# Where the constants lie in SBUF: the fp32 identity moved behind all other constants, and the transposed k's tiles rounded up to 128 bytes

## The chip, the core and the metric

The kernel runs on one core of a Trainium2 chip. Five engines run side by side, each with its own instruction stream: TensorE (PE, with its weight loads shown as PEld), VectorE (DVE), ScalarE (ACT), GpSimd (POOL) and SyncE (SP). They share the on-chip memory SBUF (128 partitions) and, but for GpSimd and the DMAs, the accumulators in PSUM. Data moves between HBM and SBUF by 16 DMA engines, which work on transfers that POOL, SP and ACT issue. The metric is the time of one execution in microseconds (us), measured on the device; the median of several runs counts.

## The reference

Sparse attention with 8 heads, of which four see the last 32 positions ("local") and four see every 32nd position ("strided"), and then a feed-forward layer with ELU.

```
q, k, v: (8 batches, 8 heads, 576 positions, 64), fp32
scores = q k^T / 8
local  heads 0-3: 0 <= i - j < 32
strided heads 4-7: j <= i and j % 32 == i % 32
x = softmax(masked scores) v                 -> 4608 x 512
h = x @ w_in                                 512 x 2048
g = h if h > 0 else exp(h) - 1
out = g @ w_out                              2048 x 512, fp32
```

## The kernel before

All matmuls run in bf16. The 4608 tokens are cut into nine chunks of 512 for the two layers, and the attention runs batch by batch ahead of them. The order of the work is written out by hand: ORDER is a string of some 2,000 tokens (lines 35 to 145), and the loop at its end runs one small function for each token, so every engine's stream and every DMA's place are fixed. The tokens that matter here:

- D issues a load from POOL (load, line 267). The loads turn fp32 into bf16 on the way. qs, ks and vs are the strided heads' q, k and v, with 1024 B for each partition and head (load_runs, line 231, issued at L233). From batch 2 on, ql and kl (L243, L250) are split by position in pieces of 64 elements, 128 B each. vl (L260, L262) has pieces of 128 B too, with a block of 64 ones between any two, so its pieces start at odd multiples of 128 B within the tile. w_in and w_out come in quarters (L275, L279). One quarter of w_in, the one with columns 1536 to 2047, is loaded as two transfers.
- X issues a DMA transpose from SP (dma_T, line 594, issued at L604). From batch 2 on it writes q and k with the head dimension on the partitions: qT and kT, for strided (s) and local (l) heads, each in two tiles that alternate by batch. For batches 0 and 1, TensorE transposes instead (T, L404 and L410, L413), and copies (c, C) bring the results to the same tiles. The first transposes of batch 0 are of fp32 data and use identity_f.
- S are the scores' matmuls (L456), e the exponentials (L463), m the masks (L470, L476), O the product with v (L483 to L499 for batches 0 and 1, L519 and L526 from batch 2 on), n, r and x the division by the sums, L, a, b the first layer (L611), h, i, j, g the ELU (L619 to L639), Z the second layer (L645), o, q, t, u, Y and y the way out (copies at L651, stores from SP and ACT at L663).
- w are matmuls on zeros (L390) that keep TensorE busy while the first loads are under way. V copies 32 rows of batch 0's and 1's vl to the partitions of the position block before (L588), once the load has landed.

The constants are allocated one behind the other from one pool, in the order of the code, each rounded up to a multiple of 32 B. Up to identity, all of them have sizes that are multiples of 128 B, and the first starts at a multiple of 128. Line 185 allocates identity_f with 72 fp32 numbers, which are 288 B. Everything allocated behind it starts 32 B past a multiple of 128, until kTs0 (2656 B) and kTl0 (2368 B) shift it further. Batch 1's raw q and k lie for a while in the space of xT, and its v in that of g[1], which lie ahead of identity_f.

| tile | start before, B mod 256 | start after, B mod 256 |
|---|---|---|
| xT, g, w_in_sb, w_out_sb | 128 | 128 |
| qs, ks, ql, kl, vs, ql1, kl1 | 32 | 0 |
| vl0, vl1 | 32, 160 | 0, 128 |
| vsp | 32 | 0 |
| qTs, qTl | 160 | 128 |
| kTs0, kTs1 | 160, 64 | 128, 128 |
| kTl0, kTl1 | 0, 160 | 0, 0 |
| e, pm | 32 or 160 | 0 or 128 |
| ln, he, osb | 32 | 0 |

The addresses are those of the built programs, the same in each partition.

Of the kernel before, what the change touches and what calls it, by code (L numbers as in the profile page):

```python
# [8 lines left out]
F32 = mybir.dt.float32  # L9
BF16 = mybir.dt.bfloat16  # L10
# [6 lines left out]
D = 64  # L17
HG = 4
NS = 8
RS = S // NS  # L20
RP = 80
LQ = 96
LB = S // LQ
LN = LQ // NS
PRE = STRIDE
# [123 lines left out]
def kernel(  # L149
# [18 lines left out]
    consts = ctx.enter_context(tc.tile_pool(name="consts", bufs=1))  # L168
# [13 lines left out]
    w_out_sb = consts.tile([128, MC, d_model], BF16, tag="w_out_sb", name="w_out_sb")  # L182
    zero = consts.tile([128, CHUNK], BF16, tag="zero", name="zero")
    identity = consts.tile([128, 128], BF16, tag="identity", name="identity")
    identity_f = consts.tile([RS, RS], F32, tag="identity_f", name="identity_f")
    ones = consts.tile([128, D], BF16, tag="ones", name="ones")


# [17 lines left out]
    KLW = PRE + 2 * S  # L206

    qT = [{c: consts.tile([128, 2 * NS * RP], BF16, tag=f"qT{c}{i}", name=f"qT{c}{i}")
           for c in "sl"} for i in range(2)]
    kT = [{c: consts.tile([128, n], BF16, tag=f"kT{c}{i}", name=f"kT{c}{i}")  # L210
           for c, n in (("s", KSW), ("l", KLW))} for i in range(2)]
    dist = consts.tile([RS, RS], I32, tag="dist", name="dist")
    same = consts.tile([RS, RS], I32, tag="same", name="same")
# [1 line left out]
    mask_s = consts.tile([RS, RS], BF16, tag="mask_s", name="mask_s")  # L215
    mask_1 = consts.tile([128, NS, LN], BF16, tag="mask_1", name="mask_1")
    mask_l = consts.tile([128, 2, NS, 3, LN], BF16, tag="mask_l", name="mask_l")

    def rawof(nm, b):
        if b == 1:  # L220
            return raw1[nm]
        return odd[nm] if b % 2 and nm in odd else raw[nm]

    def runs(x, b, h, n):

        rows = RP if (b * H + h + n - 1) * S + RP * NS <= B * H * S else RS
        return rows, bass.AP(x.tensor, x.offset + (b * H + h) * S * D,
                             [[NS * D, rows], [S * D, n], [1, NS * D]])
# [65 lines left out]
    for eng, n, x in ((nc.sync, 0, q), (nc.scalar, 1, k)):  # L294
        for i in range(2):
            rows, in_ = runs(x, 0, HG, 2)
            f = NS * D // 2
            eng.dma_start(out=half(stage[0:rows, n * 4 * f:(n + 1) * 4 * f], i),
                          in_=in_[:, :, i * f:(i + 1) * f])
# [12 lines left out]
        identity_f, identity_f, compare_op=ALU.is_equal, fill=0.0,  # L312
# [281 lines left out]
    def dma_T(what, b):  # L594
        nm, c = what
        n = HG * NS // 2
        t = (qT if nm == "q" else kT)[int(b) % 2][c]
        in_ = rawof(what, int(b))
        if what == "kl":
            t, in_ = t[:, PRE:], in_[:, 0:HG * LB * D]  # L600
        else:
            t = t[:, 0:n * RP]
        p = LQ if what == "kl" else RP
        nc.sync.dma_start_transpose(out=t.rearrange("c (n p) -> c n p", p=p), in_=in_)  # L604
# [75 lines left out]
    def out_piece(ch, kk, i):  # L680
# [11 lines left out]
        "C": lambda *a: copy_T(nc.scalar.copy, *a),  # L692
        "S": scores, "e": exp_s, "m": mask, "O": pv, "n": log_sums, "r": recip, "x": write_x,
        "V": copy_vloc, "W": copy_vstr, "D": load, "X": dma_T,
        "a": lambda ch, m, bk: l1(ch, m, (2, 3), bk), "b": lambda ch, m: l1(ch, m, (0, 1)),
        "L": lambda ch, m, bk: l1(ch, m, (2, 3, 0, 1), bk), "h": exp_h,
# [39 lines left out]
```

## Time and profile before

| what | us |
|---|---|
| median of 3 runs | 308.76 |
| lowest, highest | 307.34, 308.96 |
| the profiled execution | 308.0 |
| its span in the profile | 306.3 |
| TensorE busy in it | 293.8 |

The profile follows one execution. Its page gives the busy time of each engine, 40 slices of the span with the busy tenths of each engine and of the DMA engines, the chain of work that ended last, and groups of instructions by line. A group's line reads: line, engine, operation, output<-input, number; then the busy us and the mean ns of one; then the idle time ahead of it and what ended that. A timeline's line reads: start, length, instruction, and in brackets the idle time of the engine ahead of it and what released it. In answers on DMAs, q0 holds the transfers that POOL issues, q1 those of SP, q10 those of ACT; a packet is one piece with contiguous bytes, counted by the bytes that it writes, and a queue's share is the time of its packets over that of 16 engines (packets overlap, so it can exceed 100%).

### The profile page before, as it was taken

Reading aid. Unit: us, or ns where it says so; the run is one execution under the profiler, and the core shown is the slowest. Engines: PE = TensorE matmul, PEld = TensorE weight load, DVE = VectorE, ACT = ScalarE, POOL = GpSimd, SP = SyncE. Lnnn points to the kernel's source line nnn. Section 1 sums busy time; section 2 is a strip of 40 time slices with the busy share of each in tenths; the row PEclk is TensorE's granted clock in tenths of the full one; section 3 lists DMA queues with packets and bytes.
Section 4 is the critical chain, followed back from the end, with each engine's and each line's share of the span. In section 5 each row is a group of like instructions: output and inputs, shape, how many; then the busy total and the mean of one; then the engine's idle time right before and its main releaser. Section 6 shows DMA issues by size and latency. Waiting matters only on the chain.

```text
span 306.3 us, 6207 instructions
## 1 busy us (share of the span) xinstructions
PE 293.8 (96%) x2294; PEld 147.6 (48%) x2333; DVE 224.1 (73%) x442; ACT 223.3 (73%) x402; POOL 81.0 (26%) x112
## 2 busy tenths in 40 slices
PE   8979999979999999999999999999999999999995
PEld 4644455435444455445544454455444444444444
DVE  6658948878579977998689868966699367996020
ACT  2858669669879898897998997978997569642011
POOL 8832434063294007043092742000000000000000
PEclk9999999999999999999999999999999999999999
DMA  8999999999999999999999999961120110110143
GB/s 165 177 205 206 206 194 153 135 169 189 131 121 158 172 183 179 159 134 135 169 155 210 128 139 129 112 140 35 34 72 0 36 34 0 36 35 0 36 137 103
DMA packets 107373, 37.62 MB, mean 123 GB/s; under 512 B 89168, under 2 KB 102864, under 8 KB 107344
## 3 DMA queue, kind: packets, MB, share of 16 engines
q0 software_dynamic: 69744, 19.47, 67.0%
q1 hardware_dynamic: 36836, 16.93, 31.2%
q10 hardware_dynamic: 764, 0.84, 0.9%
q8 instruction: 18, 0.29, 0.4%
q14 instruction: 11, 0.09, 0.1%
HBM read 39.53 MB, written 9.44 MB: 160 GB/s over the span
## 4 chain that ended last, share of the span: by engine, by line
PE 73%; DMA 12%; DVE 6%; POOL 3%; issue 3%; ACT 3%; POOLq 0%; ACTq 0%
PE ps L645 34%; PE ps L611 31%; DMA vl<-in_v_dram 8%; DMA kTs<-ks 4%; PE ps L456 3%; DVE g L639 2%; PE ps L526 2%; DVE he L628 2%; PE ps L519 1%; PE ps L675 1%; ACT he L619 1%; DVE xT L584 1%; POOL vs L233 1%; DVE g L637 1%; ACT e L463 1%
## 5 line engine op out<-in xcount | busy, mean ns | idle before, releaser
L645 PE MATMUL ps<-w_out_sb,g 128*128 128x512 bf16 x541 | 130.7, 379 | 1.3 <-issue 0.6
L611 PE MATMUL ps<-xT,w_in_sb 128*128 128x512 bf16 x558 | 129.5, 379 | 1.5 <-issue 0.3
L619 ACT ACTIVATE he<-ps 128x512 f32<-128x512 f32 x144 | 80.4, 597 | 25.2 <-PE ps L611 24.2
L611 PEld LDWEIGHTS <-w_in_sb 128*128 128x128 bf16 x576 | 55.0, 98 | 64.2 <-issue 0.7
L645 PEld LDWEIGHTS <-g 128*128 128x128 bf16 x560 | 50.8, 98 | 54.2
L639 DVE TENSOR_TENSOR g<-he,ps 128x512 bf16<-128x512 bf16 x103 | 68.4, 682 | 1.6
L584 DVE TENSOR_TENSOR xT<-ps,ln 64x576 bf16<-64x576 f32 (+1 forms) x64 | 42.6, 678 | 22.6 <-ACT ln L559 21.2
L628 DVE TENSOR_SCALAR he<-he 128x512 bf16<-128x512 f32 x103 | 43.7, 437 | 12.6 <-ACT he L619 11.9
L463 ACT ACTIVATE e<-ps 72x576 bf16<-72x576 f32 (+1 forms) x64 | 38.7, 646 | 12.7 <-PE ps L456 9.3
L554 ACT ACTIVATE ln<-ps 64x576 f32<-64x576 f32 (+1 forms) x64 | 36.3, 584 | 9.4 <-PE ps L519 5.3
L559 ACT ACTIVATE ln<-ln 64x576 f32<-64x576 f32 (+1 forms) x64 | 38.4, 622 | 1.2
L637 DVE SCALAR_TENSOR_TENSOR g<-he,ps 128x512 bf16<-128x512 bf16 x41 | 27.5, 681 | 5.2 <-ACT he L626 5.1
L626 ACT ACTIVATE he<-he 128x512 bf16<-128x512 f32 x41 | 25.4, 630 | 1.8 <-DVE g L639 1.1
L250 POOL DMA_DIRECT2D kl<-in_k_dram x24 | 18.1, 767 | 21.4 <-DMA vl<-in_v_dram 11.0
L651 ACT COPY osb<-ps 128x512 f32<-128x512 f32 x17 | 9.9, 583 | 17.3 <-PE ps L645 12.6
L651 DVE COPY osb<-ps 128x512 f32<-128x512 f32 x18 | 12.3, 686 | 13.5 <-PE ps L645 12.3
L243 POOL DMA_DIRECT2D ql<-in_q_dram x24 | 20.1, 844 | 4.7 <-DMA ks<-in_k_dram 1.7
L476 DVE TENSOR_TENSOR pm<-e,mask_l 128x576 bf16<-128x576 bf16 x32 | 14.2, 455 | 7.7 <-ACT e L463 6.8
L470 DVE TENSOR_TENSOR pm<-e,mask_s 72x576 bf16<-72x576 bf16 x32 | 14.2, 449 | 4.4 <-ACT e L463 4.1
L233 POOL DMA_DIRECT2D ks<-in_k_dram x7 | 4.6, 663 | 30.0 <-DMA kTs<-ks 28.1
L233 POOL DMA_DIRECT2D vs<-in_v_dram x8 | 5.2, 648 | 27.5 <-DVE vsp L591 26.6
L519 PEld LDWEIGHTS <-vsp 72*128 72x128 bf16 x192 | 9.3, 98 | 5.5 <-DVE pm L470 0.5
(89 smaller groups left out, 158.1 us busy)
## 6 DMA issues: line engine op xcount, KB each, us to landing
out_dram<-osb SPq DMA_DIRECT2D x29, 144.0 KB
vl<-in_v_dram POOLq DMA_DIRECT2D x8, 288.0 KB, 12.9
w_out_sb<-in_moe_w_out_dram POOLq DMA_DIRECT2D x4, 512.0 KB, 17.0
kl<-in_k_dram POOLq DMA_DIRECT2D x24, 72.0 KB, 7.8
ql<-in_q_dram POOLq DMA_DIRECT2D x24, 72.0 KB, 11.9
qs<-in_q_dram POOLq DMA_DIRECT2D x5, 320.0 KB, 9.7
ks<-in_k_dram POOLq DMA_DIRECT2D x5, 320.0 KB, 7.8
vs<-in_v_dram POOLq DMA_DIRECT2D x5, 320.0 KB, 8.3
```

The costliest lines, as they stand in the source:

```text
L463: nc.scalar.activation(e[0:R], tiles.pop(("S", key, u))[0:R], ACT.Exp, scale=scale)
L554: nc.scalar.activation(t, s_ps, ACT.Ln)
L559: nc.scalar.activation(t, t, ACT.Exp, scale=-1.0)
L584: nc.vector.tensor_mul(dst, o_ps, rc)
L611: nc.tensor.matmul(tiles["h", ch, m], lhsT=w_in_sb[:, c, m * 128:(m + 1) * 128], rhs=xT[:, c, ch * CHUNK:(ch + 1) * CHUNK], start=(c == 2) ...
L619: nc.scalar.activation(e, tiles["h", i[0], i[1]], ACT.Exp)
L626: nc.scalar.activation(e1, e, ACT.Relu, bias=1.0, scale=-1.0)
L628: eng.tensor_scalar(e1, e, scalar1=1.0, scalar2=1.0, op0=ALU.min, op1=ALU.subtract)
L637: nc.vector.scalar_tensor_tensor(dst, e1, -1.0, h, op0=ALU.mult, op1=ALU.max)
L639: nc.vector.tensor_tensor(dst, e1, h, op=ALU.max)
L645: nc.tensor.matmul(ops, lhsT=g[ch % 2][:, m, kk * 128:(kk + 1) * 128], rhs=w_out_sb[:, m, :], start=(m == 0), stop=(m == MC - 1), skip_gro ...
L651: eng(o_sb, tiles.pop(("o", int(ch), int(kk))))
```

## The change

identity_f is allocated after all other constants, with 80 columns of which 72 are used, so its 288 B become 320 B. The tiles kT are rounded up to a multiple of 64 bf16 numbers: kTs from 1328 to 1344, kTl from 1184 to 1216. The transposed write of the local k names the end of its columns (KLW), since the tile is now longer than that, and the memset of the tail of kTs (line 333) covers the 16 columns more.

```diff
-    identity_f = consts.tile([RS, RS], F32, tag="identity_f", name="identity_f")
     ones = consts.tile([128, D], BF16, tag="ones", name="ones")
...
-    kT = [{c: consts.tile([128, n], BF16, tag=f"kT{c}{i}", name=f"kT{c}{i}")
+    kT = [{c: consts.tile([128, -(-n // 64) * 64], BF16, tag=f"kT{c}{i}", name=f"kT{c}{i}")
            for c, n in (("s", KSW), ("l", KLW))} for i in range(2)]
...
     mask_l = consts.tile([128, 2, NS, 3, LN], BF16, tag="mask_l", name="mask_l")
+    identity_f = consts.tile([RS, RP], F32, tag="identity_f", name="identity_f")[:, 0:RS]
...
         if what == "kl":
-            t, in_ = t[:, PRE:], in_[:, 0:HG * LB * D]
+            t, in_ = t[:, PRE:KLW], in_[:, 0:HG * LB * D]
```

## Prediction

> **What bounds the kernel now.** I read the page first (busy shares, slices), then TensorE's idle time in stretches, then the waits, then the chain.
>
> ```profile
> span 306.3 us, 6207 instructions
> PE 293.8 (96%) x2294; PEld 147.6 (48%) x2333; DVE 224.1 (73%) x442; ACT 223.3 (73%) x402; POOL 81.0 (26%) x112
> PE   8979999979999999999999999999999999999995
> DMA  8999999999999999999999999961120110110143
> ```
>
> TensorE is busy for 293.8 of 306.3 us, so the kernel is bound by its matmuls, and no change can give more than the remaining 12.5 us. The DMA engines are full for the first two thirds, yet that matters only where TensorE waits for them. The next rows are one answer for three stretches and the tail, and then the waits that belong to them.
>
> ```profile
> 14.00:18.00 4.00, 2.06 (x26) 1.16 (x28) 2.19 (x8) 2.21 (x6) 1.07 (x2) 1.00 1.22 191
> 56.00:64.00 8.00, 6.23 (x43) 2.83 (x43) 7.77 (x15) 5.60 (x10) 1.07 (x2) 1.00 1.43 154
> 80.00:83.00 3.00, 2.74 (x27) 1.31 (x27) 1.79 (x5) 2.68 (x5) 1.57 (x3) 1.00 1.57 183
> ```
>
> The columns after the stretch and its length are busy us of PE, PEld, DVE, ACT, POOL, then the granted clock, the DMA share and GB/s. TensorE is idle for 1.94, 1.77 and 0.26 us. The instructions at these places:
>
> ```profile
> 17.17 0.31 PE L499 MATMUL ps<-pm,ones 128*64 128x288 bf16 x2 [1.74 <-DVE pm L476]
> 16.07 0.55 DVE L588 COPY vl<-vl 32x1472 bf16<-32x1472 bf16 x1 [1.78 <-DMA vl<-in_v_dram]
> 63.11 0.43 PE L456 MATMUL ps<-qTs,kTs 64*128 64x72 bf16 x16 [1.72 <-DMA kTs<-ks]
> 81.93 0.39 PE L526 MATMUL ps<-pm,vl 128*128 128x96 bf16 x5 [0.21 <-DMA vl<-in_v_dram]
> ```
>
> The first stall is named after VectorE, but VectorE itself sat 1.78 us for the load of vl. So three stalls hang on DMAs: 1.74 us on batch 0's vl, 1.72 us on batch 2's kTs, and 0.21 us on batch 2's vl. The chain of waits shows how long each transfer ran:
>
> ```profile
> 7.04 9.01 DMA vl<-in_v_dram
> 50.91 12.16 DMA kTs<-ks
> 66.15 15.74 DMA vl<-in_v_dram
> ```
>
> All that faster transfers can return is 1.74 + 1.72 + 0.21 = 3.67 us; the rest of the idle time ends on other engines or on instruction issue.
>
> **The change part by part.** No instruction is added, removed or moved: on each of the five engines both programs have the same instructions in the same order. What differs is addresses and two sizes.
>
> *Identity and tile sizes.* Before, the tile identity_f (288 B per partition) pushes all constants behind it to 32 B past a multiple of 128. After, it lies last, and ones, qs to kl1, vl, vsp, qT, kT and the working tiles behind them (e, pm, ln, he, osb) start at multiples of 128 B. xT, g, w_in_sb and w_out_sb lie at multiples of 128 B in both. That gives this trace a control group: the loads of w_in_sb, w_out_sb, and batch 1's raw tiles in xT are already aligned.
>
> *The memset of kTs's tail* grows from 60 to 68 words.
>
> ```profile
> L333 DVE MEMSET kTs<- x2: 108/108/108, 2.5 to 2.7; 128x60 uint32 x2
> L332 DVE MEMSET kTs<- x2: 82/82/82, 2.5 to 2.7; 128x28 uint32 x2
> DVE qTs L423 <- PE ps L404: 1.2, 1, 1.2
> ```
>
> 32 words more cost 26 ns, so 8 more cost 6.5 ns, twice: 13 ns. They lie ahead of VectorE's first PSUM copy, before which it sits idle for 1.2 us waiting for TensorE's transposes. Cost: nothing; without that cover 0.013 us.
>
> *Engines that read or write the moved tiles.* DVE's copy to kTl ran once to kTl0 (a multiple of 256 B) and once to kTl1 (32 B past a multiple of 128).
>
> ```profile
> L431 DVE COPY kTl<-ps x2: 758/758/758, 9.3 to 46.3; 128x576 bf16<-128x576 bf16 x2
> L611 PEld LDWEIGHTS <-w_in_sb 128*128 128x128 bf16 x576 | 55.0, 98 | 64.2 <-issue 0.7
> L526 PEld LDWEIGHTS <-vl 128*128 128x128 bf16 x144 | 8.4, 97 | 5.4 <-DMA vl<-in_v_dram 0.5 <-DVE pm L476 0.2
> ```
>
> Both copies took 758 ns. Weight loads take 98 ns from the aligned w_in_sb and 97 ns from vl, which is off. I set this at 0, with bounds of 0 too: the nearest rows differ by at most 1 ns of 98.
>
> *Loads with 1024 B per write* (POOL's L233: qs, ks, kl, ql, vs). One answer for a stretch of such loads before the change, at 32 B past, and one for a stretch of aligned tiles (w_out_sb, g, xT):
>
> ```profile
> DMA packets 845, 0.79 MB, mean 197 GB/s; under 512 B 75, under 2 KB 845, under 8 KB 845
> q0 software_dynamic: 842, 0.79, 121.2%
> DMA packets 825, 0.83 MB, mean 207 GB/s; under 512 B 23, under 2 KB 824, under 8 KB 824
> q0 software_dynamic: 824, 0.82, 123.4%
> ```
>
> The first two rows are 5 to 9 us, the other two 32 to 36 us. With 16 engines, 1024 B x 16 / 197 GB/s is 83.1 ns per packet off the boundary, and 79.1 ns on it. The upper bound of the gain is thus 4.0 ns per packet. The first stretch has 75 small completion packets and the second 23, which explains part of it; the lower bound is 0. Eight loads of 160 KB (320 KB of fp32 becomes 160 rows of 1024 B) put 8 x 160 / 16 = 80 packets on each engine ahead of vl: 0 to 0.32 us. I take the middle, 0.15 us, at the first stall.
>
> *Loads with 128 B per write* (vl L260, L262; ql L243; kl L250). Here no aligned row exists. In the next answer (12.0 to 12.4 us) nothing but batch 0's vl moves, and every write of it lies at 160 to 288 B of a 256 B stride.
>
> ```profile
> DMA packets 494, 0.06 MB, mean 158 GB/s; under 512 B 494, under 2 KB 494, under 8 KB 494
> ```
>
> 494 / 16 = 30.9 packets per engine in 400 ns: 12.96 ns each. The aligned 1024 B packet reads eight times the bytes in 79.1 ns, so an eighth of it, 9.9 ns, is a floor that alignment can't break. The bounds are 9.9 and 12.96 ns. vl has 24 x 96 = 2304 packets, 144 per engine: 0 to 0.44 us. I take 0: even with every write off the boundary the rate is close to that floor, and what is above it has to hold all of a packet's fixed cost.
>
> [...]
>
> *Transposes* (SP's L604, 256 B read per packet from qs, ks, ql, kl, 32 B past a 256 B line). From 149.9 to 150.7 us they run alone:
>
> ```profile
> q1 hardware_dynamic: 920, 0.23, 127.9%
> ```
>
> 920 / 16 = 57.5 packets in 800 ns: 13.9 ns each. Bounds: no gain, or down to the 9.9 ns above. Ahead of the stall at 63.11 stand qTs and kTs with 2 x 1280 / 16 = 160 packets per engine: 0 to 0.64 us. They took 12.16 us instead of the 2.2 us that 160 x 13.9 ns would be, since they share the engines with loads and wait for stragglers:
>
> ```profile
> DMA  6463963444344545375359979999999999999999
> DMA packets 782, 0.18 MB, mean 90 GB/s; under 512 B 757, under 2 KB 782, under 8 KB 782
> ```
>
> This is 52 to 54 us: the engines are far from full at first, although kTs is due. What ends last there is a few late engines, not the mean rate. I take 0.15 us, near the lower end. For the 0.21 us at 81.93 the same holds: 0, bound 0.21.
>
> *Stores* from osb end at 306 us. They read 2048 B, so a saved fraction at one edge is lost in the length of a packet: 0.
>
> **Sum.** 0.15 + 0.15 = 0.3 us less than this execution's 308.0 us (span 306.3 and 1.7 around it): 307.7. The three runs' median of 308.76 lies 0.76 above the profiled run; on that footing 308.5, which I forecast. With the bounds (0.32 + 0.44 + 0.64 + 0.21 = 1.61 less, or nothing) this case lies between 307.1 and 309.1.
>
> **Rivals.** *All three stalls go.* If off-line writes are what makes the late engines late, as a cost that only shows when transfers of several queues meet, the transfers end some us sooner. The first stall can then shrink only until the next piece of w_in is missing: POOL, waiting for that piece, is released by 20.12 us and TensorE uses it from 20.86, so 0.74 us.
>
> ```profile
> 20.12 0.74 POOL L279 DMA_DIRECT2D w_out_sb<-in_moe_w_out_dram  x1 [1.79 <-DMA w_in_sb<-in_moe_w_in_dram]
> 20.86 9.23 PE ps L611 x42
> ```
>
> With 1.72 and 0.21 this gives 2.67 us less: 306.1. For it: the stalls end on late engines, and a mean packet rate says nothing of those. Against it: vl's 12.96 ns with every write off the line.
>
> *kTs of batch 2 lands later.* TensorE already stands at that matmul, so each us of delay is a us of time. Transposes and loads share the engines, and quicker or slower packets shift which load is in flight when kTs is issued at 50.91. Equal loads of vl show how far such neighbours move a landing:
>
> ```profile
> DMA to landing us min/median/max: 9.0/12.7/15.7
> ```
>
> From the median to the longest are 3.0 us. A delay of 2.5 us, kTs landing at 65.6 instead of 63.1, gives 311.3. It decides from 1.5 us of delay on. For it: the order of the work was written out with these landings, and 1.72 us of idle time shows no slack there. Against it: nothing in the change makes a packet longer.
>
> *The change does not do what it says.* kT's tile for local heads is written from column 32 (64 B) on, so its transposes still start 64 B past a multiple of 128; for qs, ks, vs, ql, kl and vl the addresses do move as described. The time then is the old one, 308.8, inside the forecast case.
>
> **How the numbers follow.** The forecast case, which holds the last rival too, gets 0.45, all stalls gone 0.29, kTs later 0.26. About 0.5%, 1.54 us, is what a measurement of this kernel can tell from no change. The first case lies between 307.1 and 309.1, within that of 308.76 but for its edge; the second is 0.9% faster, the third 0.8% slower. So faster 0.29, same 0.45, slower 0.26. The range reaches from 305.6 (the second case and half a us) to 311.1 (nearly all of the third).
>
> **What would show it.** Right: 1024 B loads in the first 10 us at 200 GB/s or more, vl's packets still at 13 ns, transposes alone at 13 ns or less, and the waits for vl and kTs within 0.3 us of 1.74 and 1.72. Wrong: vl's packets near 10 ns, or the late engines between 52 and 55 us gone, or kTs landing after 64.5 us, or any copy, mask or weight load with another mean. The forecast falls as a whole if TensorE's idle time of 12.5 us changes by more than 1.5 us.

## The result, and the profile after

The changed kernel is faster: 306.32 us against 308.59 us (medians of 20 runs each), a ratio of 0.9939 with a 95% interval of 0.9916 to 0.9961. The forecast was 308.5 us. Ratios here and below leave out executions that took over 1.5% longer than the fastest of their kernel, and medians are of all.

The profiled execution of the changed kernel took 309.15 us, the longest of its 20 (305.2 to 309.15). It has to be read in parts, then. First the page and the three stretches with the stalls, columns as before:

```profile
span 307.4 us, 6207 instructions
PE 295.5 (96%) x2294; PEld 148.4 (48%) x2333; DVE 224.0 (73%) x442; ACT 223.2 (73%) x402; POOL 81.7 (27%) x112
...
PEclk9989999999999999999999999999999999999999
DMA  8999999999999999999999989931020110110143
...
q0 software_dynamic: 69744, 19.47, 64.0%
q1 hardware_dynamic: 36836, 16.93, 29.3%
```

```profile
14.00:18.00 4.00, 1.53 (x21) 0.81 (x22) 0.92 (x5) 1.72 (x5) 0.50 (x1) 1.00 1.23 194
56.00:64.00 8.00, 7.95 (x39) 3.61 (x39) 6.16 (x13) 5.59 (x13) 0.73 (x2) 1.00 1.69 166
80.00:83.00 3.00, 2.95 (x29) 1.38 (x25) 2.17 (x4) 2.98 (x7) 1.20 (x2) 1.00 1.14 146
```

In the second and third stretch TensorE is now busy for 7.95 of 8 and 2.95 of 3 us, where it was idle for 1.77 and 0.26 us. But this execution runs about 3 us late, so the matmuls that waited for kTs and vl come behind these stretches now. They don't wait there either:

```profile
64.72 0.43 PE L456 MATMUL ps<-qTs,kTs 64*128 64x72 bf16 x16
83.12 0.42 PE L526 MATMUL ps<-pm,vl 128*128 128x96 bf16 x6
```

In the first stretch TensorE is worse off than before, and the reason stands in two rows, one from the timeline and one from an answer on stretches:

```profile
18.86 0.31 PE L499 MATMUL ps<-pm,ones 128*64 128x288 bf16 x2 [3.13 <-DVE pm L476]
```

```profile
20.00:24.00 4.00, 4.00 (x27) 1.83 (x26) 2.26 (x6) 2.84 (x8) 1.49 (x3) 0.57 1.23 202
```

Batch 0's vl landed late in this execution, TensorE stood for 3.13 us instead of 1.74, and the clock granted to it then fell to 0.57 of full speed in the next 4 us. The trace has it at half speed for 3.41 us, which costs another 1.7 us (an estimate: half of 3.41).

The queues' shares changed as well. With the same packets and bytes, q0 (loads) went from 67.0% to 64.0% and q1 (transposes and stores) from 31.2% to 29.3%. These are the page's lines before:

```profile
q0 software_dynamic: 69744, 19.47, 67.0%
q1 hardware_dynamic: 36836, 16.93, 31.2%
```

To find the place of the gain I cut each span at ScalarE's first exponential (L619 in the two kernels) of each chunk, which comes at the same point of the work in all kernels. The start is at the first chunk's; the numbers are us worked out from the traces:

```
                         start  chunk 0  chunk 1  chunk 2  to the end   span
no fall of the clock in the opening
before                   22.79    32.57    34.27    31.35      185.29  306.28
e7, all off by 64 B      22.61    32.57    34.45    31.22      184.97  305.81
e10, before, reordered   22.38    32.57    34.01    32.20      185.12  306.27
e6, ql and kl off        21.98    32.57    33.35    31.21      184.95  304.06
e4, work tiles off       21.43    33.06    33.41    31.23      185.47  304.60
e5, qs, ks, vs off       21.50    32.61    33.10    31.52      185.03  303.75
e9, after, reordered     21.91    32.57    33.54    31.01      185.68  304.70
e11, after, reordered    21.80    32.57    33.03    31.01      185.65  304.06
half clock for 3.41 us in the opening
e8, all off by 32 B      24.92    32.57    34.03    31.90      185.36  308.79
e1, raw tiles off        24.29    33.01    32.84    31.48      184.99  306.61
e2, vl off               24.12    32.57    32.12    31.23      185.61  305.65
after                    26.05    32.70    32.11    31.22      185.37  307.44
e3, qT and kT off        25.56    32.77    32.11    31.11      185.48  307.03
```

From chunk 3 on, all agree within 0.8 us. With all writes of 128 B aligned, the two that start late (the changed kernel at 26.05 us, e3 at 25.56) take 63.3 and 63.2 us for chunks 1 and 2, and the four that start at 21.4 to 21.9 us take 64.0 to 64.6, so executions have to be compared within a group. The 2.3 us by which chunks 1 and 2 (about 55 to 121 us) differ between the two profiled executions, 65.6 before and 63.3 after, are therefore not the gain, though they have its size.

In the first group, the three with all loads off the boundary start at 22.4 to 22.8 us and take 65.6 to 66.2 us for chunks 1 and 2. The four with all writes of 128 B on it (e4, e5, e9, e11) start at 21.4 to 21.9 us and take 64.0 to 64.6. The means of the spans differ by 1.8 us: 0.9 at the start and 1.4 in chunks 1 and 2, less 0.5 elsewhere. In the second group, chunks 1 and 2 take 65.9 us in e8 and 63.2 to 63.3 in e3 and the changed kernel. e6 and e2, with some loads off, look like aligned ones here, though their medians don't; e6's profile is of the fastest of its twelve executions.

The fall of the clock has a part in the medians, too. Of each run the mean granted clock is known, and none lies between 0.994 and 0.997. In the six traces with 0.994 or less the clock is at half for 3.41 us somewhere from 17.5 to 23.9 us, and the eight others have no such fall. With 0.994 or less are 54 of 99 executions of the kernel before (those taken beside the experiments) and 15 of 24 of e7 and e8, but 4 of 20 of the changed kernel and 12 of 36 of e3, e4 and e11; e6 (1 of 12) and e10 (3 of 12) don't fit. Among executions without the fall, the medians on the same chip are 307.56 us before and 305.53 (e3) and 305.55 (e4), 306.93 before and 305.50 (e5), 307.11 before and 305.47 (e11). So 1.4 to 2.0 us are won without the clock's help, and the rest of the 2.3 us can come from the rarer fall. That alignment makes the fall rarer is not shown.

### The profile page after: what moved, and what is told of

Read it like the earlier page. It is cut to its first block, busy times and chain, and to the rows that moved or that the text cites. A ratio compares the mean times of both kernels' runs of the same rounds, so it can differ in the third digit from the quotient of the medians.

```text
span 307.4 us, 6207 instructions
## 1 busy us (share of the span) xinstructions
PE 295.5 (96%) x2294; PEld 148.4 (48%) x2333; DVE 224.0 (73%) x442; ACT 223.2 (73%) x402; POOL 81.7 (27%) x112
## 3 DMA queue, kind: packets, MB, share of 16 engines
q1 hardware_dynamic: 36836, 16.93, 29.3%
## 4 chain that ended last, share of the span: by engine, by line
PE 81%; DVE 6%; ACT 4%; DMA 3%; issue 3%; POOL 2%; ACTq 0%; DVEq 0%; POOLq 0%
PE ps L611 36%; PE ps L645 36%; DMA vl<-in_v_dram 3%; PE ps L456 3%; PE ps L519 2%; DVE g L639 2%; PE ps L526 2%; DVE he L628 1%; ACT ln L554 1%; PE ps L675 1%; ACT he L619 1%; ACT e L463 1%; DVE xT L584 1%; ACT ln L559 1%; PE ps L499 1%
## 5 line engine op out<-in xcount | busy, mean ns | idle before, releaser
L619 ACT ACTIVATE he<-ps 128x512 f32<-128x512 f32 x144 | 80.4, 596 | 25.7 <-PE ps L611 24.0
L651 ACT COPY osb<-ps 128x512 f32<-128x512 f32 x17 | 9.9, 584 | 17.3 <-PE ps L645 10.6
L243 POOL DMA_DIRECT2D ql<-in_q_dram x24 | 21.0, 878 | 4.7 <-DMA ks<-in_k_dram 1.3
L651 DVE COPY osb<-ps 128x512 f32<-128x512 f32 x18 | 12.2, 684 | 13.5 <-PE ps L645 12.3
L476 DVE TENSOR_TENSOR pm<-e,mask_l 128x576 bf16<-128x576 bf16 x32 | 14.2, 455 | 7.9 <-ACT e L463 7.1
L470 DVE TENSOR_TENSOR pm<-e,mask_s 72x576 bf16<-72x576 bf16 x32 | 14.2, 448 | 3.8 <-ACT e L463 3.2
## 6 DMA issues: line engine op xcount, KB each, us to landing
w_out_sb<-in_moe_w_out_dram POOLq DMA_DIRECT2D x4, 512.0 KB, 17.5
```

Source lines behind the costliest of these rows:

```text
L619: nc.scalar.activation(e, tiles["h", i[0], i[1]], ACT.Exp)
L651: eng(o_sb, tiles.pop(("o", int(ch), int(kk))))
```

## The experiments

All ratios are to the kernel before, from runs on the same chip. Pads are unused tiles that shift what is allocated behind them.

**Which tiles? (e1 to e4)** In the changed kernel, one group of tiles at a time goes back to 32 B past a multiple of 128. e1 shifts the raw tiles of q, k and v:

```diff
+    pad0 = consts.tile([RS, 8], F32, tag="pad0", name="pad0")
     raw = {nm: consts.tile([RP, HG * NS * D], BF16, tag=nm, name=nm) for nm in ("qs", "ks", "ql")}
...
+    pad1 = consts.tile([RS, 24], F32, tag="pad1", name="pad1")
     vl_t = [consts.tile(
```

> Only qs, ks, ql, kl, vs, ql1 and kl1 go back to 32 B past a multiple of 128 (a pad of 32 B ahead of them and one of 96 B behind); all other tiles stay at multiples of 128. Theory R (the gain of the change comes from these tiles: 1024 B and 128 B loads write them, and the transposes read 256 B rows from them, which costs when several queues meet): ratio to the kernel before 0.998 to 1.000, q0's share of the 16 engines back to about 67% and q1's to about 31%. Theory T (the transposes' targets) and theory W (working tiles, stores): ratio 0.994, shares as with the whole change (64.0% and 29.3%). Theory N (no alignment matters; the 0.6% are landings that moved): ratio anywhere from 0.992 to 1.000, shares unrelated to it.

Measured: 307.35 us, ratio 0.9969 (0.9937 to 1.0002). q0's share went back to 67.8% and q1's to 31.3%, as theory R had it; the time lies half way, a little below its 0.998 to 1.000.

e2 has the same two pads around vl0, vl1 and vsp.

> Only vl0, vl1 and vsp go back to 32 B past a multiple of 128. Their loads write 128 B each; vl0's writes then cross a 256 B line and vl1's don't. If 128 B writes off the boundary cost something when queues meet: ratio to the kernel before 0.996 to 0.998, with more of the 128 B packets slow (q0's share 65 to 67%). If they cost nothing, as the 12.96 ns of batch 0's vl say: ratio 0.994, share 64%. Theory N: anything from 0.992 to 1.000.

Measured: 307.02 us, ratio 0.9960 (0.9930 to 0.9989), q0's share 66.4%. It fits the first case: about a third of the gain is lost, though its interval overlaps that of the whole change.

e3 has them around qT and kT.

> Only qT and kT, the targets of the DMA transposes, go back to 32 B past a multiple of 128. Theory T (the transposes' writes are what got cheaper): ratio to the kernel before 0.997 to 1.000 and q1's share near 31%. Theories R and W: ratio 0.994, q1's share 29.3%. Theory N: anything from 0.992 to 1.000.

Measured: 305.60 us, ratio 0.9934 (0.9900 to 0.9968), q1's share 29.5%, q0's 62.8%. Nothing is lost: where the transposes write doesn't matter here, and theory T falls.

e4 has one pad behind mask_l, so e, pm, ln, he and osb move.

> Only the tiles behind the constants (e, pm, ln, he, osb) go back to 32 B past a multiple of 128; no load and no transpose touches them, the stores read osb. Theory W (engines' operands or the stores' 2048 B reads): ratio to the kernel before 0.997 to 1.000, and the mean of the masks, clamps or ELUs or of the 2048 B packets changes. Theories R and T: ratio 0.994, all means of VectorE and ScalarE within 2 ns of those with the whole change. Theory N: anything from 0.992 to 1.000.

Measured: 306.49 us, ratio 0.9938 (0.9908 to 0.9968), shares 63.9% and 28.4%. Nothing is lost: theory W falls.

**Which transfers, and which boundary? (e5 to e8)** e5 splits e1: qs, ks and vs stand together behind a pad of 32 B, and a pad of 96 B follows, so ql, kl and the rest are aligned.

```diff
+    pad0 = consts.tile([RS, 8], F32, tag="pad0", name="pad0")
+    raw = {nm: consts.tile([RP, HG * NS * D], BF16, tag=nm, name=nm) for nm in ("qs", "ks")}
+    raw["vs"] = consts.tile([RP, HG * NS * D], BF16, tag="vs", name="vs")
+    pad1 = consts.tile([RS, 24], F32, tag="pad1", name="pad1")
+    raw["ql"] = consts.tile([RP, HG * NS * D], BF16, tag="ql", name="ql")
```

> Only qs, ks and vs lie 32 B past a multiple of 128: their loads write 1024 B at a time, and qs and ks are read by transposes. ql, kl, ql1, kl1, vl and all else are at multiples of 128. If what costs is writes of 128 B off the boundary: ratio to the kernel before 0.994, q0's share 63 to 64%. If what costs is the transposes' reads of 256 B rows off a 256 B line: half of the transposes are off, so half of what raw_off lost comes back, ratio near 0.9955, q1's share 30 to 31%.

Measured: 305.58 us, ratio 0.9941 (0.9908 to 0.9975): nothing is lost. In its profile q0's share is 66.4% all the same, against the expectation, so that share alone doesn't tell the time.

e6 is the other half: qs, ks and vs aligned, then a pad of 32 B, ql, kl, ql1 and kl1, and a pad of 96 B ahead of vl.

> Only ql, kl, ql1 and kl1 lie 32 B past a multiple of 128: from batch 2 on their loads write 128 B at a time, and the other half of the transposes reads them. If what costs is writes of 128 B off the boundary: ratio to the kernel before 0.997 (as with all raw tiles off), q0's share 66 to 68%. If what costs is the transposes' reads: ratio near 0.9955 as for the kernel with qs, ks and vs off, and the two agree.

Measured: 306.63 us, ratio 0.9979 (0.9949 to 1.0008), q0's share 65.1%. About two thirds of the gain is gone by the ratio, in line with the 0.997 expected; the share is less than the 66 to 68% expected. Transposes read both halves, so if their reads were what costs, e5 and e6 should agree; the ratios are 0.9941 and 0.9979. The intervals overlap. Without the fall of the clock, eleven executions of each on the same chip are left, with medians of 305.50 and 306.63 us, and eight of e6's lie above all of e5's. Together with e2, where no transpose reads what was moved, this points to the writes of 128 B.

e7 shifts everything behind ones by 64 B, e8 by 32 B, with kT's new sizes and identity_f last in both.

```diff
+    pad0 = consts.tile([RS, 16], F32, tag="pad0", name="pad0")
     raw = {nm: consts.tile([RP, HG * NS * D], BF16, tag=nm, name=nm) for nm in ("qs", "ks", "ql")}
```

> All tiles behind ones lie 64 B past a multiple of 128, with the new sizes of kT. If the boundary that counts is one of 64 B or less: ratio to the kernel before 0.994, q0's share near 64%. If it is 128 B or 256 B: ratio 0.998 to 1.000, q0's share near 67%.

Measured: 307.75 us, ratio 1.0013 (0.9982 to 1.0044), q0's share 69.1%. 64 B is not enough. Whether the boundary is one of 128 or of 256 B stays open: from a start 64 B off, all writes of 128 B cross a multiple of 128 B, and half of them one of 256 B as well.

> All tiles behind ones lie 32 B past a multiple of 128, identity_f stays last and kT keeps its new sizes: the change without its alignment. If alignment is the cause: ratio to the kernel before 0.998 to 1.002, shares 67% (q0) and 31% (q1). If the order of allocation or kT's sizes are: ratio 0.994.

Measured: 308.28 us, ratio 1.0014 (0.9971 to 1.0057), shares 68.8% and 31.6%. Without the alignment, the rest of the change is worth nothing.

How long the 50,496 packets of 128 B took, counted in each trace:

```
                                     over 40 ns
before                               6.1%
e8, all off by 32 B                  6.6%
e7, all off by 64 B                  4.9%
e10, before, reordered               5.9%
e1, raw tiles off                    5.1%
e2, vl off                           3.4%
e6, ql and kl off                    2.9%
after                                2.4%
e3, e4, e5                           1.2%, 2.1%, 1.8%
e9, e11 (after, reordered)           1.8%, 3.0%
e12, before without transposes       3.6%
```

A packet of 128 B takes 31 or 32 ns by the trace (several overlap). Off the boundary, 5 to 7% take over 40; with only vl or only ql and kl off, about 3%; with all of them aligned, 1.2 to 2.4%, e11 being the exception. The limit of 40 ns was set with the traces in view. At 60 ns the shares are 5.0% before and 1.7% after, but the mean length doesn't separate the kernels (35.8 ns before, 35.5 in e5). Between 50 and 121 us, where the time differs, they lie closer: 5.3% before, 4.2% after and 5.0% in e11, though 10.9% in e8. So the long packets are a sign of the alignment, not a measure of the time that it costs.

**Is it the landing of batch 2's kTs? (e9 to e11)** After e8 I noted that in each profile the span is the start of batch 2's first score matmuls plus 242.4 to 243.4 us, and took the wait for kTs ahead of them for the place that sets the time (theory K). So I moved those matmuls behind two tiles of the first layer.

```diff
-S.2s1.0.01 S.2s1.1.23 h.1.2 g.1.3 L.1.10.7 e.2s1.0 g.1.5 D.ql.3 e.2s1.1 L.1.15.5 i.1.2 h.1.10 g.1.2
+h.1.2 g.1.3 L.1.10.7 L.1.15.5
+S.2s1.0.01 S.2s1.1.23 e.2s1.0 g.1.5 D.ql.3 e.2s1.1 i.1.2 h.1.10 g.1.2
```

> The changed kernel, with batch 2's first two groups of score matmuls placed two first-layer tiles later (8 matmuls of 0.216 us, 1.7 us) on TensorE. In all profiles so far the span is the start of these matmuls plus 242.4 to 243.4 us, and TensorE stood 0.7 to 1.7 us for kTs ahead of them in most. Theory K (the landing of batch 2's kTs sets the time, and alignment moved it): the stall goes, ratio to the kernel before 0.988 to 0.992, that is 0.5 to 1.7 us below the changed kernel. Rival (another chain of waits behind it takes its place): ratio 0.993 to 0.995.

Measured: 306.59 us, ratio 0.9959 (0.9934 to 0.9983): no better than the changed kernel.

> The kernel before, addresses unchanged, with the same later place of the score matmuls. Theory K: most of the stall of 1.72 us goes, ratio to the kernel before 0.993 to 0.996, and what alignment is still worth on top (e9 against this one) is less than the 0.6% it was worth alone. If alignment acts all along the kernel, e9 stays 0.6% ahead of this one. If the landing of kTs doesn't set the time: ratio 1.000.

Measured: 308.26 us, ratio 1.0010 (0.9979 to 1.0042): no gain. The stall on kTs is gone from its profile, but the timeline of TensorE shows what came in its place:

```profile
62.91 0.43 PE L457 MATMUL ps<-qTs,kTs 64*128 64x72 bf16 x16
...
66.64 3.61 PE L612 MATMUL ps<-xT,w_in_sb 128*128 128x512 bf16 x16 [0.88 <-DVE g L640]
...
81.25 0.39 PE L527 MATMUL ps<-pm,vl 128*128 128x96 bf16 x5 [0.31 <-DMA vl<-in_v_dram]
...
106.60 0.43 PE L457 MATMUL ps<-qTl,kTl 64*128 64x96 bf16 x12 [0.90 <-DMA qTl<-ql]
```

Four us later TensorE waits 0.88 us for VectorE, then for vl, then 0.90 us for batch 3's qTl. Theory K falls. In e9, with the same order and aligned tiles, the wait of 0.88 us is there too and the last two are not. The two ratios differ by 0.5%: alignment is worth about as much with the stall on kTs hidden as with it open, so it acts at several landings, those of vl and qTl among them.

e11 moves the matmuls by one tile, in the changed kernel.

> The changed kernel with the same score matmuls one first-layer tile later (4 matmuls, 0.86 us). Theory K: 0.4 to 0.9 us below the changed kernel, ratio to the kernel before 0.991 to 0.993, between the changed kernel and e9. Rival: as the changed kernel, 0.994.

Measured: 305.60 us, ratio 0.9942 (0.9908 to 0.9976), the same as the changed kernel. No version that I ran is clear of it.

**Does it take the transposes to make the loads slow? (e12)** The kernel before, with X doing nothing and the ends of qT cleared once.

```diff
-        "V": copy_vloc, "W": copy_vstr, "D": load, "X": dma_T,
+        "V": copy_vloc, "W": copy_vstr, "D": load, "X": lambda *a: None,
```

> The kernel before with all DMA transposes left out (scores from batch 2 on then use old contents of qT and kT, so the output is not the reference's). If loads of 128 B off the boundary are slow only beside transposes: hardly any 128 B packet takes over 40 ns (under 1%; 6.1% before), q0's share falls from 67% to 62% or less, and kTs's stall is gone. If they are slow by themselves or beside stores: 4% or more stay over 40 ns and q0's share stays above 65%.

Measured: 308.06 us in a single run, with the clock halved for 3.41 us as above. From its page:

```profile
q0 software_dynamic: 69744, 19.47, 64.1%
q1 hardware_dynamic: 6116, 9.26, 10.0%
```

q0's share falls to 64.1%, and 3.6% of the packets of 128 B still take over 40 ns. This lies between the two cases. So transposes are not needed for writes off the boundary to be slow. Nor is any other queue: in this trace, of the 26,697 packets of 128 B with no packet of another queue within 1 us, 3.1% take over 40 ns, and in that of the kernel before 8.8% of 11,989. In the aligned ones (after, e3, e4, e5, e9, e11) it is 0.1% or less, but in e8 and e10, which are off, it is only 0.2%, and there the long packets sit beside other queues. How much each of the others adds, these runs don't settle.

## Why the prediction was right or wrong

The time of 306.32 us is in the range, 305.6 to 311.1, but outside the case that I forecast, 307.1 to 309.1. (The upper end of that case doesn't come out of its sum, which ends at 308.76.) The change gained 0.6 to 0.7%, 2.3 us where the forecast had 0.3. The range holds because it took in the rival "all three stalls go" (0.29, 306.1 us), which had the size and the direction. That its number is so close is luck in part: in like executions without the fall of the clock the stall on kTs shrinks and doesn't go, from 1.72 us before and 1.58 in e7 to 1.24 in e4 and 0.90 in e5.

```profile
61.76 0.43 PE L457 MATMUL ps<-qTs,kTs 64*128 64x72 bf16 x16 [1.24 <-DMA kTs<-ks]
61.04 0.43 PE L459 MATMUL ps<-qTs,kTs 64*128 64x72 bf16 x16 [0.90 <-DMA kTs<-ks]
```

These two are from e4 and e5. Of the signs that were to show the forecast right, one came, vl's packets at 13 ns. The loads from 5 to 9 us moved at 183 GB/s in the changed kernel's profile, not 200 or more; the transposes stayed at 14.2 ns; and the waits for vl and kTs were 3.13 us and none.

**The step that failed is the one on loads with 128 B per write**, "I take 0". It rested on vl's 12.96 ns per packet with every write off the boundary. The measurement was right, and its use wrong. The same stretch with aligned vl, from e4 (12.2 to 12.6 us), is the same:

```profile
DMA packets 495, 0.06 MB, mean 158 GB/s; under 512 B 495, under 2 KB 495, under 8 KB 495
...
q0 software_dynamic: 495, 0.06, 247.5%
```

495 packets in 400 ns against 494: in this stretch alignment is worth nothing. In the trace before, no packet of 128 B takes over 40 ns ahead of 50 us, and 5.3% do between 50 and 121 us; the forecast costed all of these loads at the rate of that one early stretch, and gave no cost at all to those of later batches. e2 and e6 show one: with only vl or only ql and kl off, a third and two thirds of the gain are lost. How a write off the boundary comes to cost time is not shown. I had written the cost "that only shows when transfers of several queues meet" down as the rival's mechanism and argued against it with the rate of a stretch in which only one load moved.

**The transposes alone** were to fall from 13.9 to 13 ns or less. In the changed kernel, from 114.5 to 115.1 us:

```profile
DMA packets 677, 0.17 MB, mean 289 GB/s; under 512 B 677, under 2 KB 677, under 8 KB 677
...
q1 hardware_dynamic: 677, 0.17, 127.5%
```

and before, from 149.9 to 150.5 us:

```profile
DMA packets 676, 0.17 MB, mean 288 GB/s; under 512 B 676, under 2 KB 676, under 8 KB 676
...
q1 hardware_dynamic: 676, 0.17, 127.6%
```

677 / 16 packets in 600 ns are 14.2 ns in both. Rows of 256 B read from 32 B past a multiple of 256 took no longer than rows read from a multiple, and no run shows the 0.15 us that the forecast's sum has for the transposes.

**The loads with 1024 B per write** were given 0.15 us. e5, with qs, ks and vs off, has a ratio of 0.9941 against 0.9939 for the whole change: their value can't be told from 0, as the lower bound had it.

**Engines' operands, the memset and the order of allocation** at 0 were right: e3, e4 and e8.

**The stalls** were read rightly as the place of the gain but for one thing: I took the 1.72 us at kTs as a sum to be won, all of it in the rival and 0.15 in the forecast. e10 hides that stall and wins nothing. What came out of the change is an earlier landing of several transfers in a row: in like executions, 0.9 us at the start and 1.4 us over chunks 1 and 2.

**The opening** was forecast to gain 0.15 us. TensorE's stall there was 1.74 us before, 1.68, 1.19 and 2.05 in e7, e10 and e8 (off), 1.03, 0.57 and 0.24 in e9, e4 and e5, but 2.87 and 3.13 in e3 and the changed kernel (aligned). VectorE's copy that waits for batch 0's vl starts at 15.7 to 16.6 us in the four that are off, at 14.6 to 15.2 in e4, e5, e9 and e11, and at 17.3 and 17.8 in e3 and the changed kernel. So with aligned tiles vl mostly landed about a us earlier, and in two profiles later. Why, when its rate alone is the same, stays open.

**The rival of a later kTs** didn't occur: kTs landed at 63.07 before and at 63.37 in the changed kernel's late-starting execution, where TensorE arrived after it. Its late engines are still there: of the sixteen steps in which that transfer's semaphore counts its completion, fourteen had come by 61.70 us before and 61.10 after, and the last two only by the times above.

## What to carry to other kernels

Put the targets of loads with small pieces, 128 B here, on multiples of 128 B; it costs a pad and returned 2.3 us of 308.6 here, and an odd-sized tile allocated early shifts everything behind it. Don't judge a transfer's sensitivity from one stretch in which it runs alone: batch 0's vl moved at the same rate on and off the boundary, and the long packets came later, from 50 us on. And when one execution's profile disagrees with the median, cut the span at fixed points of the work, and compare executions that started alike, before looking for a cause.

## What the runs showed of the hardware that was not expected

A stall of TensorE in the opening of 1.38 us (e1) or 1.56 us (e12) was followed by half clock for 3.41 us, while 1.74 us (before) and 1.68 us (e7) were not. By the clock's record in the traces, all six falls begin 3 or 4 times 3.413 us, the length of a fall, after the clock was first granted in full. In the changed kernel that was at 6.81 us, and the clock fell 13.653 us later, at 20.47. With the time cut in steps of 3.413 us from that first full grant on, the step just before a fall holds 1.41 to 1.83 us of TensorE's idle time. The stall of the kernel before runs from 15.43 to 17.17 us and lies across the edge of a step, at 6.21 + 3 x 3.413 = 16.45 us; the steps on its two sides hold 1.22 and 0.74 us. So that stall, though longer, left less idle time in each step than is found ahead of the falls in e1 and e12. The idle time of a step doesn't decide alone, though: one step with 1.52 us (changed kernel, ahead of the one before the fall) passed. What makes the clock fall is not shown.

Each such fall costs 1.7 us by the estimate above, as much as three quarters of this change. It is one reason why single runs of one kernel lie 4 us apart: beside the experiments, the medians of the kernel before with and without it are 1.0 to 1.2 us apart on each chip.
